# Weight low parts on VectorE, a later chunk load and a new step order in a retention and two-layer kernel

## The chip, the cores and the metric

One Trainium2 chip, one core of it. The metric is the device time of one execution in microseconds (us); of the kernel before, three executions gave 586.96 us as median, 585.64 as lowest and 587.08 as highest.

## What is computed

A retention layer (batch 2, 8 heads, 768 positions, head size 64), its output laid out as 1536 tokens of 512 numbers, and then two feed-forward layers of width 2048 one behind the other, the first with Mish, the second with ELU. q, k and v are float32; the four weight matrices arrive as float64. Cut to what matters:

```python
state = gamma[h] * state + outer(k[t], v[t])       # for each t, per batch and head
y[t] = scale * q[t] @ state
x = y.transpose(0, 2, 1, 3).reshape(1536, 512)
h = x @ w_in;  x = (h * tanh(log1p(exp(h)))) @ w_out          # moe: Mish
h = x @ w_in2; out = where(h > 0, h, exp(min(h, 0)) - 1) @ w_out2   # moe2: ELU
```

## The kernel before

**Retention.** The 768 positions of both batches are cut into 12 chunks of 128 (numbers 0 to 11, batches alternating). Chunks 0 to 3 go through `scores`, `attend` and `add_state` ahead of the main loop. Chunks 4 to 11 go through `scores64` (scores of the chunk and the new states) and `attend64` (output of the chunk), each of which issues its TensorE matmuls and returns a function `rest` that issues the work of VectorE and ScalarE behind them. For each chunk GpSimd makes a scaled k (`scale_k`, L187, tile kd) that `scores64` needs and a scaled q (`scale_q`, L202, tile qd) that `attend64` needs. From chunk 4 on there is one buffer for kd and one for qd.

**Feed-forward.** The tokens are 3 blocks of 512; each layer has 16 chunks of 128 hidden units; so there are 2 x 3 x 16 = 96 tiles. Step n of the main loop issues `up(n)` (L396: 12 matmuls 128x512, into tile h) and `down(n - 3)` (L453: 12 matmuls into the accumulators a), with the activation between them. All products are made from high and low parts: hi times hi, lo times hi, hi times lo. Steps 0 to 4 also carry the scores and outputs of chunks 4 to 7, because from step 6 on `up` needs block 1, which is made of these four chunks:

| step | TensorE in order |
|---|---|
| 0 | up(0), scores64 of chunk 4 |
| 1 | up(1), attend64 of 4, scores64 of 5 |
| 2 | up(2), attend64 of 5, scores64 of 6 |
| 3 | up(3), attend64 of 6, down(0), scores64 of 7 |
| 4 | up(4), attend64 of 7, down(1) |

**Weights.** Each of the 64 weight halves is fetched as raw 64-bit words (`fetch`, L109, tile st, four buffers), turned into float32 by two ScalarE operations (`dec_fields`, L116 and L118) and two VectorE operations (`dec_join`, L127 and L133), and then split by `dec_split`: ScalarE copies the high part (L146, tiles w0h, w1h), GpSimd subtracts to get the low part (L147, tiles w0l, w1l). `dec_join` issues the fetch of the half that takes the freed buffer. w0 is what `up` needs, w1 what `down` needs.

**Order.** The program's order is written out by hand; each engine works through its own instructions in that order, and each waits at its head for what it needs. All DMAs are issued by SyncE (SP) in one queue, with eight completion semaphores in turn. What matters below: on VectorE the order of the parts of steps 0 to 4; on GpSimd the order of kd, qd and low parts; on SP the order of chunk loads (`load_chunk`: L167 qk, L172 kv), decay tables (`load_tab`: L208) and weight halves.

"Half 3" below is the weight half with place 3 in the order of need; "kd of chunk 6" is what `scale_k(6)` writes.

Of the kernel before, what the change touches and what calls it, by code (L numbers as in the profile page):

```python
# [9 lines left out]
F32 = mybir.dt.float32  # L10
# [4 lines left out]
ALU = mybir.AluOpType  # L15
# [8 lines left out]
NCH = B * CPB  # L24
# [11 lines left out]
LAG = 3  # L36
# [7 lines left out]
def retention_then_two_ffn(  # L44
# [7 lines left out]
    nc = tc.nc  # L52
# [86 lines left out]
    def dec_split(k):  # L139
        f = parts.pop(k)  # L140
        n, i = halves[k]
        pl = late["w"] if n % (GRP + EXTRA) >= GRP else wpool
        hi, lo = wt[n, i] = tuple(
            pl.tile([P, HC], F32R, tag=f"w{i}{z}", name=f"w{i}{z}") for z in "hl"
        )
        nc.scalar.copy(out=hi, in_=f)  # L146
        nc.gpsimd.tensor_tensor(out=lo, in0=f, in1=hi.bitcast(F32), op=ALU.subtract)  # L147


    ct = const.tile([P, N_CT], F32, name="ct")  # L150
# [14 lines left out]
    def load_qk(c):  # L165
        t = qk_p.tile([P, 2, NPAIR, P], F32, tag="qk", name="qk")
        nc.sync.dma_start(out=t.rearrange("p a j t -> p (a j t)"), in_=qkv[c, :, :2 * DM])  # L167
        return t

    def load_kv(c):  # L170
        t = kv_p.tile([P, 2, H, D], F32, tag="kv", name="kv")
        nc.sync.dma_start(out=t.rearrange("p a h d -> p (a h d)"), in_=qkv[c, :, 2 * DM:])  # L172
        return t

    def load_chunk(c):
        raw[c] = (load_qk(c), load_kv(c))
# [28 lines left out]
    def load_tab(i):  # L205
        tabs[i] = qd_p.tile([P, NPAIR, P], F32, tag="tab", name="tab", bufs=2)
        at = N_CT + (i - 2) * N_TQ
        nc.sync.dma_start(  # L208
            out=tabs[i].rearrange("p j t -> p (j t)"), in_=consts[:, at:at + N_TQ]
        )  # L210
# [176 lines left out]
    hs, es, gs, accs, acc_ps = {}, {}, {}, {}, {}  # L387
# [24 lines left out]
    def mish(n):  # L412
        h = hs.pop(n)
        gh = gpool.tile([P, TB], F32R, tag="gh", name="gh")
        gl = gpool.tile([P, TB], F32R, tag="gl", name="gl")
        nc.scalar.activation(out=gh, in_=h, func=AF.Mish)  # L416
        nc.scalar.activation(out=h, in_=h, func=AF.Mish)  # L417
        nc.vector.tensor_tensor(out=gl, in0=h, in1=gh.bitcast(F32), op=ALU.subtract)  # L418
        gs[n] = (gh, gl)

    def elu_a(n):
        h = hs[n]
# [62 lines left out]
    with tc.manual_schedule():  # L485
        nc.scalar.preload_act_table_set("mish")
        for s in states:
            nc.vector.memset(s, 0.0)
        qk0 = load_qk(0)
        nc.sync.dma_start(out=ct[:, :N_MASK], in_=consts[:, :N_MASK])  # L490
        raw[0] = (qk0, load_kv(0))
        qk1 = load_qk(1)
        nc.sync.dma_start(out=ct[:, N_MASK:], in_=consts[:, N_MASK:N_CT])
        raw[1] = (qk1, load_kv(1))
        for c, tag in ((2, "xh1"), (3, "xl1")):
            both = xpool.tile([P, KT, TB], F32R, tag=tag, name=tag).bitcast(F32)
            qk, kv = (both[:, 2 * a:2 * a + 2] for a in range(2))
            nc.sync.dma_start(
                out=qk.rearrange("p a n -> p (a n)"), in_=qkv[c, :, :2 * DM]
            )  # L500
            raw[c] = (
                qk.rearrange("p a (j t) -> p a j t", t=P),
                kv.rearrange("p a (h d) -> p a h d", d=D),
            )
        def load_early_kv(c):
            nc.sync.dma_start(
                out=raw[c][1].rearrange("p a h d -> p (a h d)"), in_=qkv[c, :, 2 * DM:]
            )

        fetch()  # L510
        load_early_kv(2)
        load_early_kv(3)
        fetch()
        started = done = 0
        N = len(tiles)

        def room(k, now):
            if k >= NHALF:
                return False
            n, i = halves[k]  # L520
            old = n - GRP - (EXTRA if "w" in late else 0)
            return old < 0 or last_use[old] + LAG * i <= now

        ta, th, tb = ("a0", "a1"), ("h", "h"), ("a2", "a3")
        for i in range(3):
            warm = psa.tile([P, NPAIR, P], F32, tag=f"a{i}", name="warm")
            nc.tensor.matmul(warm, states[0][:, 0], states[0], start=True, stop=True)
        scale_k(0)
        scores(0, ta)()
        scale_k(1)  # L530
        scores(1, th)()
        for c, tags in ((0, tb), (1, th)):
            rests = attend(c, tags[0]), add_state(c, tags[1])
            for rest in rests:
                rest()
        load_chunk(4)
        fetch()
        load_chunk(5)
        load_tab(2)
        fetch()  # L540
        load_chunk(6)
        scale_q(2)
        scale_q(3)
        scores(2, ta)()
        scores(3, th)()
        dec_fields(0)
        dec_join(0)
        scale_k(2)

        lower = mask[half[1]].rearrange("p r j t -> p (r j) t")  # L550
        nc.gpsimd.tensor_copy(lower[:, :, half[0]], lower[:, :, half[1]])
        scale_k(3)
        rests = attend(2, tb[0]), attend(3, tb[1]), add_state(2, "h"), add_state(3, "h")
        rests[0]()
        dec_split(0)
        rests[1]()
        dec_fields(1)
        dec_join(1)
        scale_k(CPT)
        dec_split(1)  # L560
        rests[2]()
        rests[3]()
        dec_fields(2)
        scale_q(CPT)
        dec_join(2)
        done, joined, started, credit = 2, 3, 3, 0.0

        load_tab(3)
        steps = {0: [(scores64, 4, ta)], 3: [(attend64, 6), (scores64, 7)], 4: [(attend64, 7)]}
        for n in (1, 2):  # L570
            steps[n] = [(attend64, n + 3, tb), (scores64, n + 4, ta)]
        for c in range(2 * CPT, NCH):
            n = FIRST + 2 * (c - 2 * CPT)
            steps[n], steps[n + 1] = [(scores64, c)], [(attend64, c)]
        for n in range(N + LAG):
            todo = steps.get(n, [])
            rests = []
            if n < N:
                up(n)
                if todo:  # L580
                    f, *args = todo[0]
                    rests.append(f(*args))
            full = down(n - LAG) if n >= LAG else []
            for f, *args in todo[1:]:
                rests.append(f(*args))
            first_layer = n < N and tiles[n][0] == 0
            if first_layer:
                mish(n)
            elif n < N:
                elu_a(n)  # L590
            if 1 <= n <= N and tiles[n - 1][0] == 1:
                elu_b(n - 1)
            if full and not full[0][1]:
                for e in full:
                    evacuate(*e)
            for (f, c, *_), rest in zip(todo, rests):
                if f is scores64 and c + 1 < NCH:
                    scale_k(c + 1)
                rest()
                if f is attend64 and c + 3 < NCH:  # L600
                    load_chunk(c + 3)
                if f is attend64 and c + 1 < NCH:
                    scale_q(c + 1)
                    if c % B and (c + 1) // B + 1 < CPB:
                        load_tab((c + 1) // B + 1)
            for k in range(done, joined):
                dec_split(k)
            done = joined
            if full and full[0][1]:
                for e in full:  # L610
                    evacuate(*e)
            if 1 <= n <= N and tiles[n - 1][0] == 1:
                split(n - 1)
            if any(f is attend64 and c == NCH - 1 for f, c, *_ in todo):
                actx.close()
                late["acc"] = ctx.enter_context(pool("acc12", 1))
                late["m"] = ctx.enter_context(pool("tmp2", 2))
                late["w"] = ctx.enter_context(pool("w2", EXTRA))
            if later:
                later.pop(0)()  # L620
            dec_join(*range(joined, started))
            joined = started
            ahead = range(started, min(started + 2 * GRP, NHALF))
            credit += max([1.0] + [
                (k - started + 1) / max(need[k] - n - 2, 0.5) for k in ahead
            ])
            credit = min(credit, 2.0)
            while credit >= 1 and room(started, n):
                dec_fields(started)
                started += 1  # L630
                credit -= 1


def _consts():
# [54 lines left out]
```

## Time and profile before

| | |
|---|---|
| median of 3 executions | 586.96 us (585.64 to 587.08) |
| the profiled execution | 587.08 us, its span 585.3 us, granted clock 0.994 |
| TensorE (PE) busy | 568.0 us, 97% of the span |
| VectorE (DVE) busy | 320.4 us, 55% |
| ScalarE (ACT) busy | 282.1 us, 48% |
| GpSimd (POOL) busy | 201.6 us, 34% |

The span runs from the first to the last instruction, and what the time has beyond it (1.8 us) lies around it. An engine's busy time leaves out what its sequencer does. PEclk is the share of full speed that TensorE was granted. The profile also says of an instruction how long its engine was idle before it and what ended that.

### The profile page before, as it was taken

What the parts mean: (1) busy time and instruction counts of PE and PEld (TensorE: products, weight loads), DVE (VectorE), ACT (ScalarE), POOL (GpSimd) and SP (SyncE); (2) the same over time, 40 slices, a digit from 0 to 9 for tenths busy, and PEclk for the clock granted to TensorE, in tenths of its full rate; (3) what the DMA queues carried; (4) which work ended last, traced back from release to release, by engine and by line L of the source; (5) the groups of instructions that cost most, each with busy time, mean ns of one, the idle gap of its engine ahead of it and who ended that gap; (6) DMA issues with size and microseconds to landing.
All of it is one profiled execution on the core that took longest, in us unless ns stands there. A gap on an engine that the chain in (4) does not pass through costs nothing.

```text
span 585.3 us, 8785 instructions
## 1 busy us (share of the span) xinstructions
PE 568.0 (97%) x3510; PEld 466.5 (80%) x3510; DVE 320.4 (55%) x432; ACT 282.1 (48%) x506; POOL 201.6 (34%) x151
## 2 busy tenths in 40 slices
PE   7967999999999999999999999999999999999997
PEld 5756788888888888888888888888888888888885
DVE  3857755432655553310775996234797774534524
ACT  1555546344654652222665684434875753233331
POOL 2644433301222222110361595221565552222221
PEclk9988999999999999999999999999999999999999
DMA  8968642202242332000233232000333100100101
GB/s 326 394 237 271 199 144 74 74 1 72 77 140 76 106 108 73 0 1 0 97 120 109 72 108 73 1 0 1 109 109 108 37 0 1 72 1 0 73 0 72
DMA packets 15304, 51.70 MB, mean 88 GB/s; under 512 B 1696, under 2 KB 1696, under 8 KB 15264
## 3 DMA queue, kind: packets, MB, share of 16 engines
q1 hardware_dynamic: 15264, 51.15, 25.1%
q8 instruction: 27, 0.44, 0.3%
q14 instruction: 13, 0.11, 0.1%
HBM read 48.00 MB, written 3.15 MB: 87 GB/s over the span
## 4 chain that ended last, share of the span: by engine, by line
PE 88%; DVE 1%; POOL 0%; ACT 0%; issue 0%; POOLq 0%
PE a L453 44%; PE h L396 43%; PE y L348 1%; DVE acc L466 0%; PE y L355 0%; PE sc L304 0%; PE sc L311 0%; POOL w0l L147 0%; DVE y L370 0%; DVE xl L374 0%; ACT t L367 0%; ACT xh L372 0%; POOLq L147 0%
## 5 line engine op out<-in xcount | busy, mean ns | idle before, releaser
L396 PE MATMUL h<-xh,w0h 128*128 128x512 f32 x384 | 103.8, 392 | 2.5 <-ACT w0h L146 2.5
L409 POOL TENSOR_TENSOR gl<-m,gh 128x512 fp32r<-128x512 f32 x48 | 69.6, 1449 | 106.1 <-ACT gh L408 106.1
L396 PE MATMUL h<-xh,w0l 128*128 128x512 f32 x384 | 103.9, 393 | 2.0 <-POOL w0l L147 1.9
L418 DVE TENSOR_TENSOR gl<-h,gh 128x512 fp32r<-128x512 f32 x48 | 33.2, 691 | 130.8 <-ACT h L417 126.9
L396 PE MATMUL h<-xl,w0h 128*128 128x512 f32 x384 | 103.0, 390 | 0.0
L426 ACT ACTIVATE e<-c 128x512 f32<-128x512 f32 x48 | 30.4, 633 | 123.3 <-DVE c L425 123.3
L147 POOL TENSOR_TENSOR w0l<-f,w0h 128x512 fp32r<-128x512 f32 x32 | 42.7, 1337 | 135.1 <-ACT w0h L146 126.0
L425 DVE TENSOR_SCALAR c<-h 128x512 f32<-128x512 f32 x48 | 33.1, 690 | 101.8 <-PE h L396 101.7
L416 ACT ACTIVATE gh<-h 128x512 fp32r<-128x512 f32 x48 | 28.6, 597 | 121.3 <-PE h L396 121.3
L396 PEld LDWEIGHTS h<-xh,w0l 128*128 128x128 f32 x384 | 72.2, 189 | 18.5 <-POOL w0l L147 3.7
L396 PEld LDWEIGHTS h<-xh,w0h 128*128 128x128 f32 x384 | 71.8, 188 | 17.9 <-ACT w0h L146 3.0
L396 PEld LDWEIGHTS h<-xl,w0h 128*128 128x128 f32 x384 | 72.5, 189 | 15.3
L453 PE MATMUL a<-gh,w1h 128*128 128x512 f32 x192 | 75.8, 395 | 0.0
L453 PE MATMUL a<-gl,w1h 128*128 128x512 f32 x192 | 74.8, 390 | 0.0
L453 PE MATMUL a<-gh,w1l 128*128 128x512 f32 x192 | 74.8, 390 | 0.0
L453 PE MATMUL a<-w1h,gh 128*128 128x512 f32 x192 | 74.7, 389 | 0.0
L453 PE MATMUL a<-w1l,gh 128*128 128x512 f32 x192 | 74.7, 389 | 0.0
L453 PE MATMUL a<-w1h,gl 128*128 128x512 f32 x192 | 74.7, 389 | 0.0
L133 DVE SCALAR_TENSOR_TENSOR f<-f,st 128x512 int32<-128x512 int32 x64 | 69.7, 1098 | 3.8
L127 DVE SCALAR_TENSOR_TENSOR st<-st 128x512 int32<-128x512 int32 x64 | 71.3, 1123 | 0.6 <-ACT st L118 0.6
L147 POOL TENSOR_TENSOR w1l<-f,w1h 128x512 fp32r<-128x512 f32 x32 | 45.7, 1429 | 61.5 <-ACT w1h L146 48.4
L116 ACT ACTIVATE f<-st 128x512 f32<-128x512 f32 x64 | 42.8, 668 | 10.1 <-DMA st<-w 6.2
(80 smaller groups left out, 691.8 us busy)
## 6 DMA issues: line engine op xcount, KB each, us to landing
st<-w SPq DMA_DIRECT2D x64, 512.0 KB, 3.6
qk<-qkv SPq DMA_DIRECT2D x10, 512.0 KB, 7.6
kv<-qkv SPq DMA_DIRECT2D x10, 512.0 KB, 8.2
out<-acc SPq DMA_DIRECT2D x12, 256.0 KB, 2.1
xh<-qkv SPq DMA_DIRECT2D x2, 512.0 KB, 9.4
xl<-qkv SPq DMA_DIRECT2D x2, 512.0 KB, 10.0
tab<-consts SPq DMA_DIRECT2D x4, 256.0 KB, 8.6
ct<-consts SPq DMA_DIRECT2D x1, 512.0 KB, 5.7
```

The source lines that it names most:

```text
L116: nc.scalar.activation(out=f, in_=t[:, :, 1].bitcast(F32), func=AF.Copy, scale=2.0 ** -112)
L127: nc.vector.scalar_tensor_tensor(out=t[:, :, 1], in0=t[:, :, 1], scalar=-(2 ** 31), in1=t[:, :, 0], op0=ALU.bitwise_and, op1=ALU.bitwise_or,)
L133: nc.vector.scalar_tensor_tensor(out=f, in0=f, scalar=3, in1=t[:, :, 1], op0=ALU.logical_shift_left, op1=ALU.bitwise_or,)
L147: nc.gpsimd.tensor_tensor(out=lo, in0=f, in1=hi.bitcast(F32), op=ALU.subtract)
L348: nc.tensor.matmul(y[r][sl, far, j], state[m][sl, j], qd[sl, j, half[m]], start=j == 0 and far == 1, stop=far == 1, skip_group_check=True,)
L396: nc.tensor.matmul(h, u[:, k * P:(k + 1) * P], v[:, k], start=i == 0, stop=i == len(passes) - 1)
L409: nc.gpsimd.tensor_tensor(out=gl, in0=g, in1=gh.bitcast(F32), op=ALU.subtract)
L416: nc.scalar.activation(out=gh, in_=h, func=AF.Mish)
L418: nc.vector.tensor_tensor(out=gl, in0=h, in1=gh.bitcast(F32), op=ALU.subtract)
L425: nc.vector.tensor_scalar(out=c, in0=h, scalar1=0.0, scalar2=None, op0=ALU.min)
L426: nc.scalar.activation(out=e, in_=c, func=AF.Exp)
L453: nc.tensor.matmul(a, l, r, start=first and i == 0, stop=last and i == 2)
```

## The change

Five edits. (1) The low parts of weights (L147) are made by VectorE in place of GpSimd. (2) `mish` no longer issues the low part of its result at once but hands it back; the loop issues it behind the chunk steps, except in a later step that carries two of them. (3) In steps 0 to 2 the chunk steps' `rest` functions, with the `scale_k`, `scale_q` that go with them, are issued in reversed order: `scores64` ahead of `attend64`. (4) The load of chunk 6, and decay table 3 with it, moves from ahead of the loop to the end of step 0. (5) The other chunk loads move from behind their `attend64` to the end of the step.

```diff
@@ dec_split
-        nc.gpsimd.tensor_tensor(out=lo, in0=f, in1=hi.bitcast(F32), op=ALU.subtract)
+        nc.vector.tensor_tensor(out=lo, in0=f, in1=hi.bitcast(F32), op=ALU.subtract)
@@ mish
-        nc.vector.tensor_tensor(out=gl, in0=h, in1=gh.bitcast(F32), op=ALU.subtract)
-        gs[n] = (gh, gl)
+        def rest():
+            nc.vector.tensor_tensor(out=gl, in0=h, in1=gh.bitcast(F32), op=ALU.subtract)
+            gs[n] = (gh, gl)
+        return rest
@@ ahead of the loop
         load_tab(2)
         fetch()
-        load_chunk(6)
...
-        load_tab(3)
@@ in the loop over n
-                mish(n)
+                low = mish(n)
...
-            for (f, c, *_), rest in zip(todo, rests):
+            pairs = list(zip(todo, rests))
+            if n < LAG:
+                pairs.reverse()
+            elif first_layer and len(todo) > 1:
+                low()
+                low = None
+            for (f, c, *_), rest in pairs:
                 if f is scores64 and c + 1 < NCH:
                     scale_k(c + 1)
                 rest()
-                if f is attend64 and c + 3 < NCH:
-                    load_chunk(c + 3)
                 if f is attend64 and c + 1 < NCH:
                     scale_q(c + 1)
                     if c % B and (c + 1) // B + 1 < CPB:
                         load_tab((c + 1) // B + 1)
+            if first_layer and low:
+                low()
             for k in range(done, joined):
                 dec_split(k)
...
+            if n == 0:
+                load_chunk(6)
+                load_tab(3)
+            for f, c, *_ in todo:
+                if f is attend64 and c + 3 < NCH:
+                    load_chunk(c + 3)
```

What this does to the order on the engines shows at three places. In all of them a name's number is that of its buffer or load.

GpSimd, from the start of the main loop. Before: low parts w0l stand between kd and qd. The kd rows are those of chunks 5, 6 and 7, the qd rows those of chunks 4, 5 and 6.

```order
L202 TENSOR_TENSOR qd_338<-qk_206,tab_216 128x512
L187 TENSOR_TENSOR kd_398<-kv_214,ct_94 128x512
L147 TENSOR_TENSOR w0l_406<-f_335,w0h_405 128x512
L202 TENSOR_TENSOR qd_516<-qk_212,tab_216 128x512
L187 TENSOR_TENSOR kd_518<-kv_222,ct_94 128x512
L202 TENSOR_TENSOR qd_638<-qk_220,tab_344 128x512
L187 TENSOR_TENSOR kd_642<-kv_514,ct_94 128x512
```

The same place now, for the same chunks:

```order
L202 TENSOR_TENSOR qd_334<-qk_206,tab_216 128x512
L187 TENSOR_TENSOR kd_391<-kv_214,ct_94 128x512
L187 TENSOR_TENSOR kd_500<-kv_411,ct_94 128x512
L202 TENSOR_TENSOR qd_518<-qk_212,tab_216 128x512
L187 TENSOR_TENSOR kd_624<-kv_537,ct_94 128x512
L202 TENSOR_TENSOR qd_640<-qk_409,tab_413 128x512
```

The low part is gone, and qd of chunk 5 stands behind kd of chunk 6, qd of chunk 6 behind kd of chunk 7: each kd waits for the kv load of its chunk.

SP's queue, from the fetch of half 3 on. Before, chunk 6 (qk_220, kv_222) is loaded right behind it and chunk 7 (qk_512, kv_514) ahead of halves 7 and 8.

```order
L109 DMA st_218<-w 128x1024
L167 DMA qk_220<-qkv 128x1024
L172 DMA kv_222<-qkv 128x1024
L109 DMA st_259<-w 128x1024
L109 DMA st_323<-w 128x1024
L109 DMA st_342<-w 128x1024
L208 DMA tab_344<-consts 128x512
L167 DMA qk_512<-qkv 128x1024
L172 DMA kv_514<-qkv 128x1024
L109 DMA st_528<-w 128x1024
L109 DMA st_531<-w 128x1024
```

Now:

```order
L109 DMA st_218<-w 128x1024
L109 DMA st_255<-w 128x1024
L109 DMA st_319<-w 128x1024
L109 DMA st_338<-w 128x1024
L167 DMA qk_409<-qkv 128x1024
L172 DMA kv_411<-qkv 128x1024
L208 DMA tab_413<-consts 128x512
L109 DMA st_524<-w 128x1024
L109 DMA st_527<-w 128x1024
L167 DMA qk_535<-qkv 128x1024
L172 DMA kv_537<-qkv 128x1024
```

Chunk 6 now stands behind halves 4, 5 and 6, and chunk 7 behind halves 7 and 8, whose fetches wait until VectorE has joined halves 3 and 4 in step 1.

VectorE, from the join of half 1 to the first scores of step 0 (at). Before:

```order
L133 SCALAR_TENSOR_TENSOR f_318<-f_318,st_122 128x512
L277 TENSOR_TENSOR compact0_97<-st_292,state0_95 64x256 x2
L277 TENSOR_TENSOR compact1_98<-st_301,state1_96 64x256 x2
L127 SCALAR_TENSOR_TENSOR st_210<-st_210 128x512
L133 SCALAR_TENSOR_TENSOR f_335<-f_335,st_210 128x512
L418 TENSOR_TENSOR gl_394<-h_346,gh_393 128x512
L319 TENSOR_TENSOR at_400<-sc_359,ct_94 128x256
```

Now:

```order
L133 SCALAR_TENSOR_TENSOR f_314<-f_314,st_122 128x512
L147 TENSOR_TENSOR w0l_324<-f_314,w0h_323 128x512
L277 TENSOR_TENSOR compact0_97<-st_288,state0_95 64x256 x2
L277 TENSOR_TENSOR compact1_98<-st_297,state1_96 64x256 x2
L127 SCALAR_TENSOR_TENSOR st_210<-st_210 128x512
L133 SCALAR_TENSOR_TENSOR f_331<-f_331,st_210 128x512
L319 TENSOR_TENSOR at_393<-sc_353,ct_94 128x256
```

The low part of half 1 stands ahead of the states and of the join of half 2, and Mish's low part no longer stands ahead of at.

## Rows read from the trace of the kernel before

**Rows 1.** Busy time by stretch; columns are in the header line.
```profile
core 0: us, PE busy (x) PEld busy (x) DVE busy (x) ACT busy (x) POOL busy (x), PEclk, DMA share, GB/s
30.00:32.00 2.00, 2.00 (x114) 1.93 (x110) 0.00 (x0) 0.03 (x1) 2.00 (x2) 1.00 1.03 412
...
34.90:42.70 7.80, 3.81 (x125) 3.84 (x127) 7.23 (x14) 5.21 (x12) 1.31 (x1) 0.78 0.28 102
...
39.00:42.50 3.50, 3.50 (x113) 3.50 (x116) 3.50 (x5) 2.11 (x5) 1.31 (x1) 0.52 0.11 26
...
45.50:49.50 4.00, 4.00 (x11) 2.92 (x12) 3.96 (x7) 2.04 (x4) 2.50 (x2) 0.57 0.96 252
...
80.00:575.00 495.00, 495.00 (x2552) 409.15 (x2552) 264.75 (x339) 244.47 (x434) 164.37 (x117) 1.00 0.18 59
```

**Rows 2.** Waits, 0 to 100 us: total us, times, longest.
```profile
PE y L348 <- DVE state L326: 5.0, 2, 4.1
PE h L396 <- ACT w0h L146: 2.5, 1, 2.5
...
PE h L396 <- POOL w0l L147: 1.9, 2, 1.4
```

**Rows 3.** Groups by line and shape, VectorE: busy us, mean ns.
```profile
L127 DVE SCALAR_TENSOR_TENSOR st<-st 128x512 int32<-128x512 int32 x64 | 71.3, 1123 | 0.6 <-ACT st L118 0.6
L133 DVE SCALAR_TENSOR_TENSOR f<-f,st 128x512 int32<-128x512 int32 x64 | 69.7, 1098 | 3.8
...
L418 DVE TENSOR_TENSOR gl<-h,gh 128x512 fp32r<-128x512 f32 x48 | 33.2, 691 | 130.8 <-ACT h L417 126.9 <-PE sc L311 3.8
```

**Rows 4.** Timeline of GpSimd: start, duration, idle before.
```profile
22.57 1.05 POOL L187 TENSOR_TENSOR kd<-kv,ct 128x512 f32<-128x512 f32 x1 [1.02 <-DMA kv<-qkv]
...
27.55 1.29 POOL L202 TENSOR_TENSOR qd<-qk,tab 128x512 f32<-128x512 f32 x1 [1.36 <-DMA tab<-consts]
```

**Rows 5.** Timeline of VectorE.
```profile
22.59 1.57 DVE L133 SCALAR_TENSOR_TENSOR f<-f,st 128x512 int32<-128x512 int32 x1
24.08 1.72 DVE L277 TENSOR_TENSOR compact<-st,state 64x256 f32<-64x256 f32 x4
...
26.77 0.69 DVE L133 SCALAR_TENSOR_TENSOR f<-f,st 128x512 int32<-128x512 int32 x1
...
28.77 0.41 DVE L326 TENSOR_TENSOR state<-sc,compact 128x256 f32<-128x256 f32 x1
```

**Rows 6.** Timeline of all engines, steps 0 to 3.
```profile
24.19 0.62 ACT L146 CAST w0h<-f 128x512 fp32r<-128x512 f32 x1 [2.36 <-DVE f L133]
...
29.32 0.24 PE L348 MATMUL y<-qd,state 64*64 64x64 f32 x1 [0.98 <-DVE state L326]
...
31.21 0.66 PE L311 MATMUL sc<-kv,kd 64*64 64x64 f32 x31
...
38.89 0.24 PE L348 MATMUL y<-qd,state 64*64 64x64 f32 x1 [4.05 <-DVE state L326]
...
50.02 0.27 PE L348 MATMUL y<-qd,compact 64*64 64x64 f32 x1
```

**Rows 7.** Timeline of SP's queue: issues (x2: the pair's start).
```profile
41.07 2.03 SPq L109 DMA_DIRECT2D st<-w  x2
...
43.66 0.38 SPq L172 DMA_DIRECT2D kv<-qkv  x1
...
49.81 0.93 SPq L109 DMA_DIRECT2D st<-w  x2
...
52.13 0.38 SPq L172 DMA_DIRECT2D kv<-qkv  x1
```

**Rows 8.** DMA issues at 41.1, 43.7 and 52.1: size, us to landing.
```profile
st<-w SPq DMA_DIRECT2D x1, 512.0 KB, 3.5
...
kv<-qkv SPq DMA_DIRECT2D x1, 512.0 KB, 8.5
...
kv<-qkv SPq DMA_DIRECT2D x1, 512.0 KB, 6.6
```

## Prediction

> **What bounds the kernel now.** I read the busy time by stretch first: from 80 to 575 us TensorE is busy for all of 495 us at full clock, while VectorE has 264.75 us of work there [rows 1]. So nothing in the main part waits for VectorE or GpSimd, and the change is decided before 80 us. Next the waits of TensorE in the first 100 us: 5.0 us for the states that VectorE makes, 2.5 us for a high part of weights, 1.9 us for low parts from GpSimd [rows 2], 9.4 us in all that a better order could win. The timeline says where: attend64 of chunk 5 idles 4.05 us before it starts at 38.89, because VectorE had the rest of chunk 4's output ahead of chunk 5's states; attend64 of chunk 6 starts at 50.02 [rows 6]. Twice the clock drops: 0.52 from 39.0 to 42.5, 0.57 from 45.5 to 49.5, each right behind a TensorE idle stretch of 4.05 and 2.5 us [rows 1, 2, 6]. The prediction follows the starts of the chunk outputs, 29.32, 38.89 and 50.02, into the changed order.
>
> **The change part by part.**
>
> *Low parts on VectorE.* 64 instructions of 128x512. No row shows this form on VectorE; the nearest are 691 ns for a subtraction that reads one operand from PSUM, and 1098 to 1123 ns, the means of the two joins, which read two operands from SBUF [rows 3]. I take 0.69 us alone, and 1.1 us as the upper bound. The joins show what the gap is: one of them takes 0.69 us alone, and 1.57 us where a GpSimd operation (1.05 us from 22.57) started just before it: it ended 0.54 us behind that one's end [rows 4, 5]. So a VectorE instruction with two SBUF operands waits out a GpSimd instruction that started first. In the main part VectorE gets 64 x 0.69 = 44 us and gives back up to 64 x (0.43 + 0.41) = 54 us of such waiting, as GpSimd has less to do. I cost it at nothing there: what hides it is TensorE's 495 us against 265 of VectorE. That cover would be gone only if VectorE nearly doubled.
>
> *The same, ahead of chunk 4.* The low part of half 1 waits for ScalarE's copy, which ends at 24.19 + 0.62 = 24.81 [rows 6]. On VectorE the low part then runs to 25.5, and behind it stand the four state operations (1.72 us, which began at 24.08 [rows 5]), now to 27.2, and the join of half 2. Its first half ends at 27.8, but GpSimd's qd of chunk 4 asks at 27.55, when its table lands [rows 4], and starts before the second half can: 27.8 + 1.29 = 29.1, and the second half ends 0.54 us later, at 29.6, where before it ended at 26.77 + 0.69 = 27.46 [rows 5]. That is 2.1 us late. Mish's low part no longer stands behind it (0.69 us won), so attend64 of chunk 4 starts at about 30.75 and not at 29.32: 1.4 us later.
>
> The Trainium skill's page "SBUF — State Buffer", section "Who interferes with whom", has this as a rule: a VectorE instruction with two SBUF inputs contends with a GpSimd instruction that reads SBUF, and the later one blocks until the first is through. The trace agrees (1.57 us against 0.69). It speaks against this change, since every low part on VectorE now has two SBUF inputs. By the rule this piece is worth 1.4 us; if the second half went first, it would be 0.3 us and the sum below 1.1 us lower.
>
> *Reversed chunk steps.* The states of chunk 5 no longer wait for chunk 4's output. Before, scores64 of chunk 5 ended at 31.21 + 0.66 = 31.87 [rows 6], now 1.4 us later, at 33.3; VectorE can make the states (1.5 us) by 34.9; up(2) ended at 38.89 - 4.05 = 34.84, now 36.2. The 4.05 us wait for VectorE is gone. What is late next: qd of chunk 5 stands behind kd of chunk 6 on GpSimd, and that waits for kv of chunk 6.
>
> *Chunk 6 behind halves 4 to 6.* The fetch of half 6 waits for the join of half 2, so SP issues it at 29.65, and qk and kv of chunk 6 behind it. A lone transfer lands 3.5 us after its issue [rows 8]. With 412 GB/s [rows 1] each further 512 KB takes 1.27 us, so kv lands at 29.65 + 3.5 + 2.5 = 35.7 at best. Then kd (1.05) and qd (1.29) [rows 4]: attend64 of chunk 5 starts at 38.2 at best. Later bursts were slower: kv was the fourth transfer, and landed 43.66 + 8.5 - 41.07 = 11.1 and 52.13 + 6.6 - 49.81 = 8.9 us after the first issue [rows 7, 8], where the full rate would give 3.5 + 3.8 = 7.3. With such a delay attend64 starts at about 40. I take 39, so as before: the wait of 4 us is turned into one for qd.
>
> *Chunk 7 behind halves 7 and 8.* These fetches wait for VectorE's joins of halves 3 and 4 in step 1. The work in front of them (states, chunk 4's output, Mish's low part, the joins) is the same set that VectorE worked through from 34.9 to 42.7, 7.23 us busy in 7.8 [rows 1]. It now begins at 33.35 and takes about 7.5 us, so the second join ends at 40.85, the first at 40.2, and SP issues half 7 then (41.07 before [rows 7]). kv of chunk 7 is the fourth transfer: 7.3 us later at full rate, 8.9 and 11.1 by the two bursts. I take 10.0, the mean of the bursts, since this burst too starts from an idle queue: 50.2. GpSimd then makes kd of chunk 7 and only behind it qd of chunk 6: 50.2 + 0.1 + 1.05 + 1.29 = 52.6. So attend64 of chunk 6 starts at 52.6 and not at 50.02: **2.6 us later**. up(3) ended by 50.02 before, part of it at half clock, and nothing in front of it starts later now; so qd sets the start, and what up(3) wins is lost in front of attend64.
>
> *Behind that.* Low parts of up(4) and up(5) cost 1.9 us of waiting [rows 2]. In step 3 VectorE still has the states of chunk 7 ahead of them, in step 4 only 0.69 us of Mish: I take 0.7 us of the 1.9 as won, 0 and 1.9 as bounds. TensorE idles for 3 to 4 us ahead of attend64 of chunk 6; behind both earlier stops of that size about 3.4 us ran at half clock, which would cost 1.7 us here, or nothing if the stop is shorter. I take 0.4.
>
> **Sum.** 2.6 - 0.7 + 0.4 = +2.3 us on the profiled execution's 587.08 us (span 585.3 and 1.8 around it): **589.4 us**. The profiled execution lies 0.12 us above the median, which I leave aside.
>
> **Rivals.**
>
> 1. *The loads are in time and the removed waits are removed (faster).* If the join of half 2 were not held up by qd, everything from 29.3 on is 1.1 to 1.4 us earlier, and with a burst at full rate kv of chunk 7 lands at 39 + 7.3 = 46.3 and attend64 of chunk 6 starts at 48.7, 1.3 us earlier; with 0.7 to 1.9 us of low parts won and no half clock behind it, the sum is -2.0 to -3.2 us: 584.3. For it: 9.4 us of waits on VectorE, ScalarE and GpSimd that the new order attacks, all seen in the rows. Against it: both conditions have to hold, and a queue that lands 512 KB at 1.27 us is seen only in the first 35 us.
>
> 2. *The new wait is there, but short (no change).* The join is late as I say, but the burst runs at the full rate: kv of chunk 7 at 40.2 + 7.3 = 47.5, attend64 of chunk 6 at 49.9, so 0.1 us earlier, and 0.7 us won behind it: 586.3. It decides against my forecast when the fourth transfer lands less than about 8.3 us after the first issue.
>
> 3. *VectorE becomes the bound of the main part (slower).* Per weight half it now has two joins and a low part, 3 x 0.69 = 2.07 us alone, against 1.12 + 1.10 = 2.22 us before [rows 3]; so its load hardly grows, and a loss would need most of its instructions to collide with GpSimd. At 0.4 us more for each of 64 low parts it is 26 us of VectorE time in 495, still under the cover. I give it little.
>
> **How the numbers follow.** About 0.3%, 1.8 us, is what a measurement of this kernel can tell from no change: same is 585.2 to 588.7 us. Chances: the forecast (a late qd of chunk 6) 0.52, rival 1 0.20, rival 2 0.26, rival 3 0.02. So slower 0.54, same 0.26, faster 0.20. The forecast's own range goes from 588.0 (burst of 8.9 us) to 592 (11.1 us, an issue up to 1 us later because kd or qd of GpSimd holds up the joins of halves 3 and 4, and the full 1.7 us of half clock). With the other cases the range is 584.3 to 592.0; a win beyond rival 1's -3 us and a loss beyond 5 us are left out.
>
> **What would show it.** In the changed profile attend64 of chunks 5 and 6 (L348) should wait for POOL qd (L202), and POOL kd (L187) for the DMA kv, at about 35 and 50 us. The join of half 2 (third L133) should take about 1.7 us and end near 29.6. attend64 should start near 30.7, 39 and 52.6. Half 7 should be fetched at 40.2, and kv of chunk 7 land near 50. L147 on VectorE should take 0.69 us or a little more in the mean, the two joins fewer than 1.0 us, and TensorE should stay full from 80 to 575. I am wrong if attend64 of chunk 6 starts before 49.5, or if TensorE shows idle time behind 80 us.

## The result and the profile after

The changed kernel takes 592.31 us (median of 4, 591.56 to 594.39) against 586.3 us (585.47 to 587.08) of the kernel before on the same chip: 1.0103 times the time, interval [1.0082, 1.0123]. It is slower, as forecast, but by 6.0 us in the medians where 2.3 were forecast, and outside the range. The profiled execution took 591.56 us (span 589.8), 4.5 us over that of before (587.08); the working below is against that pair. The rest of the 6.0 us lies in which executions were profiled: that of the changed kernel is its fastest, 0.75 us under its median, and that of before lies 0.78 us over its own. The other three executions of the changed kernel took 0.3 to 2.8 us longer at a granted clock of 0.987 to 0.988 (0.991 in the profiled one, 0.994 before); where they lost it is not shown.

The waits of TensorE in the changed kernel, 0 to 100 us (total, times, longest) and, behind the dots, 85 to 589 us:

```profile
PE y L348 <- POOL qd L202: 6.6, 2, 5.3
PE h L396 <- ACT w0h L146: 3.7, 1, 3.7
...
PE h L396 <- DVE w0l L147: 1.1, 1, 1.1
...
PE a L457 <- ACT acc L467: 2.1, 1, 2.1
```

Beside [rows 2]: the 5.0 us for states became 6.6 us for qd, the wait for a high part grew from 2.5 to 3.7, that for low parts shrank from 1.9 to 1.1. The last line has no counterpart before: TensorE now waits in the main part, at 466 us, once.

So the loss has two pieces. up(6), the first tile of block 1, starts at 73.32 us and before at 71.25: **2.07 us** are lost in steps 0 to 5. From there to up start 444.72 (442.65 before) the distance stays 2.07; the tile that starts at 475.29 before starts at 479.80 now, 4.51 later: **2.44 us** more, lost at the end of a block of the second layer (16 steps on the same 512 tokens).

**The early piece.** The changed kernel's timeline, TensorE, GpSimd, VectorE and ScalarE; in brackets the idle time before a row and what ended it:

```profile
22.66 0.69 DVE L133 SCALAR_TENSOR_TENSOR f<-f,st 128x512 int32<-128x512 int32 x1
24.04 0.85 DVE L147 TENSOR_TENSOR w0l<-f,w0h 128x512 fp32r<-128x512 f32 x1 [0.69 <-ACT w0h L146]
...
27.29 0.69 DVE L133 SCALAR_TENSOR_TENSOR f<-f,st 128x512 int32<-128x512 int32 x1
...
28.02 1.27 POOL L202 TENSOR_TENSOR qd<-qk,tab 128x512 f32<-128x512 f32 x1 [3.68 <-DMA tab<-consts]
...
29.35 0.27 PE L348 MATMUL y<-qd,state 64*64 64x64 f32 x1 [1.31 <-POOL qd L202]
...
37.17 1.23 POOL L187 TENSOR_TENSOR kd<-kv,ct 128x512 f32<-128x512 f32 x1 [6.88 <-DMA kv<-qkv]
38.36 1.71 POOL L202 TENSOR_TENSOR qd<-qk,tab 128x512 f32<-128x512 f32 x1
...
40.12 0.37 PE L348 MATMUL y<-qd,state 64*64 64x64 f32 x1 [5.28 <-POOL qd L202]
...
43.05 0.76 ACT L367 COPY t<-y 64x256 f32<-64x256 f32 x2 [4.73 <-PE y L355]
...
44.70 0.75 DVE L319 TENSOR_TENSOR at<-sc,ct 128x256 f32<-128x256 f32 x2 [4.09 <-PE sc L311]
...
46.26 0.88 DVE L370 TENSOR_TENSOR y<-y,t 64x256 f32<-64x256 f32 x2
...
47.71 0.63 ACT L146 CAST w0h<-f 128x512 fp32r<-128x512 f32 x1
...
48.39 1.93 PE L396 MATMUL h<-xh,w0h 128*128 128x512 f32 x4 [3.74 <-ACT w0h L146]
...
49.90 1.14 POOL L187 TENSOR_TENSOR kd<-kv,ct 128x512 f32<-128x512 f32 x1 [9.83 <-DMA kv<-qkv]
51.00 1.73 POOL L202 TENSOR_TENSOR qd<-qk,tab 128x512 f32<-128x512 f32 x1
...
52.94 0.27 PE L348 MATMUL y<-qd,compact 64*64 64x64 f32 x1
```

attend64 of chunk 4 starts at 29.35, as before (29.32 [rows 6]). TensorE idles 5.28 us ahead of attend64 of chunk 5, for qd, which stands behind a kd that waited 6.88 us for its load. The scores of chunk 6 come later with it, VectorE waits 4.09 us for them, and behind its states and chunk 5's output ScalarE makes the high part of half 3 only at 47.71; so up(3) starts at 48.39 (45.43 before). The reversed order adds to that: ScalarE had copied chunk 5's output by 43.81 (t), but VectorE's next operation on it (y) stands behind the states of chunk 6 and starts at 46.26; before, y came ahead of those states, at 43.30. No kernel below undoes the reversal alone, so its price is not measured. attend64 of chunk 6 starts at 52.94 (50.02 before [rows 6]): up(3)'s matmuls end just then, and qd, ending at 52.73, is hardly ahead of them.

**The late piece.** Busy time from 430 to 480 us (columns as in [rows 1]); the kernel before:

```profile
430.00:480.00 50.00, 50.00 (x222) 41.42 (x221) 41.27 (x47) 32.81 (x58) 27.20 (x19) 1.00 0.19 64
```

and the changed kernel:

```profile
430.00:480.00 50.00, 47.85 (x211) 39.33 (x210) 42.48 (x53) 31.91 (x57) 10.58 (x9) 1.00 0.24 74
```

VectorE was already busy for 41 of 50 us here, where the 495 us of the main part gave 264.75 [rows 1]. One step of this stretch in the changed kernel (c, L429, is the first VectorE operation on a tile of `up`), then the block's end:

```profile
441.07 0.68 DVE L429 TENSOR_SCALAR c<-h 128x512 f32<-128x512 f32 x1
...
441.79 0.63 ACT L430 ACTIVATE e<-c 128x512 f32<-128x512 f32 x1 [2.15 <-DVE c L429]
...
442.99 0.60 ACT L146 CAST w0h<-f 128x512 fp32r<-128x512 f32 x1
...
443.63 0.69 DVE L147 TENSOR_TENSOR w0l<-f,w0h 128x512 fp32r<-128x512 f32 x1 [0.56 <-ACT w0h L146]
...
444.19 1.30 POOL L409 TENSOR_TENSOR gl<-m,gh 128x512 fp32r<-128x512 f32 x1 [4.31 <-ACT gh L408]
444.24 1.81 DVE L127 SCALAR_TENSOR_TENSOR st<-st 128x512 int32<-128x512 int32 x1
...
446.08 0.69 DVE L133 SCALAR_TENSOR_TENSOR f<-f,st 128x512 int32<-128x512 int32 x1
...
446.69 0.68 DVE L429 TENSOR_SCALAR c<-h 128x512 f32<-128x512 f32 x1
...
465.45 2.03 ACT L467 COPY acc<-a 128x512 f32<-128x512 f32 x4
...
466.07 0.50 PE L457 MATMUL a<-w1h,gh 128*128 128x512 f32 x1 [2.15 <-ACT acc L467]
```

From c to c it is 5.61 or 5.62 us, and TensorE needs 5.44 for a tile (32.64 us for six, 442.65 to 475.29 before). The step is a ring: ScalarE waits 2.15 us for c, makes the high part only behind its two operations on it, VectorE waits 0.56 us for that high part, GpSimd's gl then holds up the join (1.81 us where 0.69 is its time alone, ending 0.56 us behind gl, as in [rows 4, 5]), and the next c is late. At the block's end ScalarE's copies of the accumulators stand behind its late work, and TensorE, which needs the accumulators, stops for 2.15 us.

The groups of VectorE over the whole execution, changed kernel (busy us, mean ns):

```profile
L127 DVE SCALAR_TENSOR_TENSOR st<-st 128x512 int32<-128x512 int32 x64 | 69.1, 1088 | 0.7 <-ACT st L118 0.7
L133 DVE SCALAR_TENSOR_TENSOR f<-f,st 128x512 int32<-128x512 int32 x64 | 48.7, 770 | 1.7
...
L147 DVE TENSOR_TENSOR w0l<-f,w0h 128x512 fp32r<-128x512 f32 x32 | 22.2, 695 | 15.5 <-ACT w0h L146 15.4
L147 DVE TENSOR_TENSOR w1l<-f,w1h 128x512 fp32r<-128x512 f32 x32 | 21.9, 685 | 6.6 <-ACT w1h L146 6.6
```

Beside [rows 3], L133 gave back 21.0 us and L127 2.2. The low parts cost 44.1 us of work, as reckoned, and in the third column 22.0 us of waiting for ScalarE, which the reckoning did not have.

### The profile page after: what moved, and what is told of

Same layout as the page of the kernel before. It is cut to its first block, busy times and chain, and to the rows that moved or that the text cites. A ratio compares the mean times of both kernels' runs of the same rounds, so it can differ in the third digit from the quotient of the medians.

```text
span 589.8 us, 8635 instructions
## 1 busy us (share of the span) xinstructions
PE 569.9 (97%) x3510; PEld 467.6 (79%) x3510; DVE 332.6 (56%) x496; ACT 282.4 (48%) x506; POOL 108.3 (18%) x87
## 4 chain that ended last, share of the span: by engine, by line
PE 84%; DVE 7%; DMA 4%; ACT 3%; POOL 1%; issue 0%; SPq 0%; POOLq 0%
PE a L457 40%; PE h L396 40%; DVE st L127 2%; DMA kv<-qkv 2%; DMA xl<-qkv 2%; PE y L348 1%; DVE f L133 1%; ACT e L430 1%; ACT c L431 1%; DVE c L429 1%; PE sc L304 1%; DVE w0l L147 1%; PE y L355 1%; PE sc L311 1%; ACT w0h L146 1%; DVE acc L470 0%
## 5 line engine op out<-in xcount | busy, mean ns | idle before, releaser
L409 POOL TENSOR_TENSOR gl<-m,gh 128x512 fp32r<-128x512 f32 x48 | 63.2, 1316 | 206.8 <-ACT gh L408 202.5
L429 DVE TENSOR_SCALAR c<-h 128x512 f32<-128x512 f32 x48 | 33.0, 687 | 75.0 <-PE h L396 75.0
L127 DVE SCALAR_TENSOR_TENSOR st<-st 128x512 int32<-128x512 int32 x64 | 69.1, 1088 | 0.7 <-ACT st L118 0.7
L487 POOL TENSOR_TENSOR xl<-acc,xh 128x512 fp32r<-128x512 f32 x12 | 17.4, 1450 | 180.2 <-ACT xh L486 176.6
L133 DVE SCALAR_TENSOR_TENSOR f<-f,st 128x512 int32<-128x512 int32 x64 | 48.7, 770 | 1.7
L457 PEld LDWEIGHTS a<-w1h,gh 128*128 128x128 f32 x192 | 36.0, 188 | 10.1 <-ACT acc L467 2.6
```

Of the source, the lines that this page charges most:

```text
L127: nc.vector.scalar_tensor_tensor(out=t[:, :, 1], in0=t[:, :, 1], scalar=-(2 ** 31), in1=t[:, :, 0], op0=ALU.bitwise_and, op1=ALU.bitwise_or,)
L133: nc.vector.scalar_tensor_tensor(out=f, in0=f, scalar=3, in1=t[:, :, 1], op0=ALU.logical_shift_left, op1=ALU.bitwise_or,)
L409: nc.gpsimd.tensor_tensor(out=gl, in0=g, in1=gh.bitcast(F32), op=ALU.subtract)
L429: nc.vector.tensor_scalar(out=c, in0=h, scalar1=0.0, scalar2=None, op0=ALU.min)
L457: nc.tensor.matmul(a, l, r, start=first and i == 0, stop=last and i == 2)
L487: nc.gpsimd.tensor_tensor(out=xl, in0=s, in1=xh.bitcast(F32), op=ALU.subtract)
```

## The experiments

Each was timed beside the kernel before on the same chip, in three groups on three chips: the first four below against 586.67 us; qd ahead of kd, the two kernels with exchanged tags and the first with the splits against 586.39; the other four against 587.07. In the traces up(0) starts between 20.7 and 21.4 us (20.96 before, 20.80 in the changed kernel), so starts in different kernels compare to some tenths of a microsecond. In kernels that choose the engine of the low part in a line of their own, the later lines are numbered one higher (L397 is `up`).

**Low parts by layer.** Two kernels split edit (1). The changed kernel with the low parts of the second layer on GpSimd:

```diff
-        nc.vector.tensor_tensor(out=lo, in0=f, in1=hi.bitcast(F32), op=ALU.subtract)
+        eng = nc.vector if n < NFC else nc.gpsimd
+        eng.tensor_tensor(out=lo, in0=f, in1=hi.bitcast(F32), op=ALU.subtract)
```

> The changed kernel, with the low parts of the second layer's weights made by GpSimd again (first layer: VectorE). Ring theory: the loss of 6 us has two pieces, 2.1 us before 70 us (late loads, GpSimd's order) and 2.4 us or more at about 466 us, where TensorE waits for ScalarE's accumulator copies because in the second layer VectorE's low part waits for ScalarE and its join behind it for GpSimd, 5.61 us a step against TensorE's 5.44. So here the wait at 466 us is gone, the part before 70 us stays +2, and the time is 588.5 to 590. Rival (load: VectorE's extra work as such, or all of the loss before 80 us): 591.5 to 592.5, as the change.

The kernel before with only the low parts of the second layer on VectorE (the same line with `n >= NFC`):

> The kernel before, with the low parts of the second layer's weights alone made by VectorE. Ring theory: nothing changes before 80 us, one wait of TensorE for ScalarE's accumulator copies of 2 to 4 us appears in the second layer, and the time is 2.4 to 4 us above before (588.5 to 590.5). Rival (all of the loss is in the first 80 us): no difference from before, no wait there.

The first took 589.79 us, 1.0071 [1.0044, 1.0097], TensorE waits for nothing behind 85 us, and up(6) starts at 73.39. The second took 589.77 us, 1.0053 [1.0033, 1.0073], its early part is that of before (up(6) at 71.54), and it has the stop: 2.15 us at 464.29. The late piece belongs to the low parts of the second layer, alone and in either kernel. In the medians each of the two lies 3.1 us over before, 6.2 in sum, as the whole change does with 6.0. The start of c in the first of the two:

```profile
442.27 0.69 DVE L430 TENSOR_SCALAR c<-h 128x512 f32<-128x512 f32 x1 [0.99 <-PE h L397]
447.71 0.69 DVE L430 TENSOR_SCALAR c<-h 128x512 f32<-128x512 f32 x1 [0.98 <-PE h L397]
```

In that kernel VectorE has 0.98 us to spare per tile of 5.44. In the changed kernel the low part asks for 0.61 us of its time (start to start) and 0.56 of waiting. That is 1.17, so 0.19 too much: 5.63, where 5.61 was measured.

**Lock or load.** The changed kernel with gl of the second layer on VectorE too, so that GpSimd has nothing there and VectorE has more:

```diff
-        nc.gpsimd.tensor_tensor(out=gl, in0=g, in1=gh.bitcast(F32), op=ALU.subtract)
+        nc.vector.tensor_tensor(out=gl, in0=g, in1=gh.bitcast(F32), op=ALU.subtract)
```

> The changed kernel, with the second layer's low part of the activation (gl, 48 subtractions of 128x512) also on VectorE, so that GpSimd no longer takes part in the second layer's steps. Ring theory: the join no longer waits for GpSimd, a step of the ring shrinks from 5.61 to about 5.0 us, the wait at 466 us goes although VectorE has 33 us more to do: 588.5 to 590. Rival (VectorE's load as such): the wait grows, 593 to 600.

589.87 us, 1.0061 [1.0037, 1.0084], and no stop of TensorE in the main part. The changed kernel's c from the block's start, and the low part in its first step:

```profile
415.00 0.69 DVE L429 TENSOR_SCALAR c<-h 128x512 f32<-128x512 f32 x1 [2.10 <-PE h L396]
...
419.51 0.69 DVE L147 TENSOR_TENSOR w0l<-f,w0h 128x512 fp32r<-128x512 f32 x1 [2.50 <-ACT w0h L146]
...
423.65 0.68 DVE L429 TENSOR_SCALAR c<-h 128x512 f32<-128x512 f32 x1
...
457.92 0.68 DVE L429 TENSOR_SCALAR c<-h 128x512 f32<-128x512 f32 x1
463.54 0.68 DVE L429 TENSOR_SCALAR c<-h 128x512 f32<-128x512 f32 x1
```

and with gl on VectorE:

```profile
415.33 0.69 DVE L429 TENSOR_SCALAR c<-h 128x512 f32<-128x512 f32 x1 [0.66 <-PE h L396]
423.45 0.68 DVE L429 TENSOR_SCALAR c<-h 128x512 f32<-128x512 f32 x1
...
454.64 0.68 DVE L429 TENSOR_SCALAR c<-h 128x512 f32<-128x512 f32 x1
459.74 0.68 DVE L429 TENSOR_SCALAR c<-h 128x512 f32<-128x512 f32 x1
```

Counted in steps of 5.44 us from the first row, both are about 3 us late at 423.5: in the block's first step ScalarE copies accumulators ahead of the high part, and VectorE waits 2.50 us for that at the low part, with the joins behind it. With GpSimd silent the step is then 5.10 us, below TensorE's 5.44, and VectorE catches up, from 2.9 us late at 429.15 to 0.9 at 459.74; with the lock it is 5.61 and VectorE falls from 4.0 us late (429.84) to 5.0 (463.54). So the six ring steps add only 1.1 of these 5.0 us, and the block's first step 3.2; what the lock decides is that VectorE can't work them off. That makes the stop, not the number of VectorE's operations: the kernel that doesn't stop has 48 more.

**Chunk loads.** The changed kernel with edits (4) and (5) undone (chunks 6 and 7 and table 3 loaded where they were):

```diff
+        load_chunk(6)
...
+                if f is attend64 and c + 3 < NCH:
+                    load_chunk(c + 3)
...
-            if n == 0:
-                load_chunk(6)
-                load_tab(3)
-            for f, c, *_ in todo:
-                if f is attend64 and c + 3 < NCH:
-                    load_chunk(c + 3)
```

> The changed kernel, with all chunk loads and decay table 3 back where the kernel before has them. Theory of the late loads: kv of chunk 6 lands near 31 us and that of chunk 7 near 38.5, qd of chunk 5 is ready by 34.5 and attend64 of chunk 5 starts at 35 to 36 in place of 40.1; attend64 of chunk 6 starts at 44 to 47 in place of 52.9; the time before 70 us falls by 4 to 7 us, that at 466 us stays: 585 to 588. Rival (the reversed order or VectorE's own order costs it): attend64 of chunk 6 stays above 49 and the time above 590.

590.46 us, 1.0064 [1.0039, 1.009]. up(6) starts at 71.22, as before, and the stop of 2.15 us at 464 stays: without the late loads the early piece is gone. But the gain that the theory expected did not come, and the signs of the rival did: attend64 of chunk 6 started at 50.81, not at 44 to 47, and the time is above 590. attend64 of chunk 5 came at 37.48, not at 35 to 36; it waited 2.99 us for xl (the low part) of chunk 4's output, whose banks in PSUM, the memory that matmuls write to, it takes over. That is 1.41 us earlier than before, but up(3) starts 0.36 us later than before (45.79), behind a wait of 3.55 us for its high part. What the early loads win at chunk 5 is lost again in front of up(3).

**Order of kd and qd.** The changed kernel, loads still late, but GpSimd makes qd ahead of kd:

```diff
             for f, c, *_ in pairs:
-                if f is scores64 and c + 1 < NCH:
-                    scale_k(c + 1)
                 rest()
+            for f, c, *_ in todo:
+                if f is scores64 and c + 1 < NCH:
+                    scale_k(c + 1)
                 if f is attend64 and c + 1 < NCH:
                     scale_q(c + 1)
```

> The changed kernel with one edit: in a step of the first block GpSimd makes qd of the next chunk output first and kd of the next scores behind it (before this edit kd, then qd). Chunk 6 is still fetched late (its kv lands at about 37). Theory (the early loss of 2.1 us is qd of chunk 5 queued behind kd of chunk 6, which waits for kv of chunk 6): attend64 of chunk 5 no longer starts at 40.1 but at about 37.5, where the kernel with early loads had it, now ended by another wait than qd; scores64 of chunk 6 waits for kd until about 38.5; up(6) starts 1 to 2 us earlier than 73.3; the second loss stays (TensorE waits about 2 us for ScalarE's copy near 464); the whole 590 to 591. Rival (what counts is when the load itself lands, through chunk 6's own scores and states): up(6) stays at 73 or later and the whole at 592.

588.63 us, 1.0056 [1.0035, 1.0076]. Its TensorE waits:

```profile
35.71 0.29 PE L348 MATMUL y<-qd,state 64*64 64x64 f32 x2 [0.58 <-DVE xl L374]
44.41 2.08 PE L396 MATMUL h<-xh,w0h 128*128 128x512 f32 x4 [5.57 <-ACT w0h L146]
```

attend64 of chunk 5 starts at 35.71 and up(6) at 69.23, 4.1 us earlier than in the changed kernel and 2.0 earlier than before, with the loads as late as they were (kd waits for kv until 36.83), and more than the 1 to 2 us expected. The early piece needs both, a late load and a qd queued behind the kd that waits for it; the lateness alone does not cost it. The 2.16 us for ScalarE's copy remain (at 461.99).

**Both causes away.** The last kernel with the second layer's low parts on GpSimd:

> The changed kernel with both suspected causes taken away: qd of the next output ahead of kd on GpSimd, and the low parts of the second layer on GpSimd again; loads, reversed steps and first-layer low parts stay as changed. Theory (two causes, in two stages, that add): up(6) starts at about 69.2 to 70 as with the reordering alone (73.3 in the changed kernel, 71.25 before), TensorE doesn't wait near 464, and the time is 585 to 587, so no slower than before. Rival (a third cause, or one that comes back once the other is gone): 588 or more, with a wait that neither kernel showed.

585.24 us, 0.9985 [0.9962, 1.0007]: no slower than before. up(6) starts at 68.43, and nothing waits in the main part. The two causes account for the loss. What remains is the wait of up(3) for its high part (3.73 us at 43.64).

**Loads and order alone.** The changed kernel with edit (1) undone (all low parts on GpSimd):

> The changed kernel with all low parts on GpSimd again, so only the loads and the order of steps are changed. Theory (the low parts cost only in the second layer; the early loss is the order and the loads): up(6) at 73 to 74, no wait near 464, 589 to 590, as with the second layer's low parts alone on GpSimd (589.8). Rival (the first layer's low parts on VectorE gain or cost time in front of chunk 6): up(6) more than 1 us from 73.4.

594.33 us, 1.0129 [1.0113, 1.0145], no faster than the whole change, against the theory: up(6) starts only at 79.14, 5.75 us behind the kernel that differs in the first layer's low parts. Its GpSimd and TensorE:

```profile
49.51 1.04 POOL L187 TENSOR_TENSOR kd<-kv,ct 128x512 f32<-128x512 f32 x1 [9.96 <-DMA kv<-qkv]
50.51 1.71 POOL L202 TENSOR_TENSOR qd<-qk,tab 128x512 f32<-128x512 f32 x1
52.19 1.71 POOL L147 TENSOR_TENSOR w0l<-f,w0h 128x512 fp32r<-128x512 f32 x1
...
53.95 2.07 PE L396 MATMUL h<-xh,w0l 128*128 128x512 f32 x4 [3.98 <-POOL w0l L147]
```

On GpSimd the low part of up(3) stands behind the kd and qd that wait for chunk 7. So with these loads VectorE is the better place for it in the first layer, and it is the worse one in the second.

**Trying for a gain.** Four kernels attack what the traces left. First the PSUM banks: the low parts as in the first experiment, loads early, and the tags of step 2 (they name the PSUM banks that a chunk step takes) exchanged.

```diff
-        for n in (1, 2):
-            steps[n] = [(attend64, n + 3, tb), (scores64, n + 4, ta)]
+        steps[1] = [(attend64, 4, tb), (scores64, 5, ta)]
+        steps[2] = [(attend64, 5, ta), (scores64, 6, tb)]
```

> Low parts of the second layer on GpSimd again, chunk loads where they were in the kernel before, and in step 2 the PSUM tags of chunk 5's output and chunk 6's scores exchanged. With the loads early and the tags as they are, attend64 of chunk 5 started at 37.5 with a wait of 3.0 us. Theory (that rest is the reuse of the two PSUM banks of chunk 4's output, which VectorE reads only behind ScalarE's copy of half 4): with the other banks attend64 of chunk 5 starts at 35 to 36 behind up(2), with no wait of over 1 us, and up(6) starts 1 to 2 us before 71.2. Rival (VectorE's order sets it, whichever bank): start stays at 37 to 38 and up(6) at 71.2. By both there is no wait of TensorE near 464; time by the theory 584 to 586, by the rival 587.

attend64 of chunk 5 starts at 34.68, right behind up(2), so the banks did hold it; but up(3) then waits 7.31 us for its high part, up(6) starts at 72.20, and the time is 588.28 us, 1.003 [1.0013, 1.0047]. Neither the theory nor the rival had that: the wait was only moved. That leaves ScalarE's order, in which the high part of half 3 stands behind xh of chunk 5's output. The splits ahead of the chunk steps' rests, chunk 6 loaded behind half 4:

```diff
+            if 2 <= n <= 4:
+                for k in range(done, joined):
+                    dec_split(k)
+                done = joined
             pairs = list(zip(todo, rests))
```

> Low parts of the second layer on GpSimd, chunk 6 loaded behind half 4 only, the other loads as in the kernel before, and in steps 2 to 4 the splits (high parts on ScalarE, low parts) placed ahead of the chunk steps' rests. Theory (the 3.7 us wait of up(3) for the high part of its half is ScalarE's order: the copy stands behind xh of chunk 5): the wait of up(3) falls under 0.5 us, up(3) starts at about 43 and up(6) at about 69 to 70; 584 to 586 us. Rival (TensorE then waits for something else, chunk 6's states or chunk 7's load, for as long): up(6) stays at 71 and the time at 587 to 588.

582.68 us, 0.9947 [0.9923, 0.9971]: faster than both kernels. Its TensorE:

```profile
35.47 0.33 PE L349 MATMUL y<-qd,state 64*64 64x64 f32 x2 [0.72 <-POOL qd L203]
38.90 1.19 PE L397 MATMUL h<-xh,w0h 128*128 128x512 f32 x4 [0.68 <-ACT w0h L146]
42.23 0.27 PE L349 MATMUL y<-qd,compact 64*64 64x64 f32 x1 [0.31 <-POOL qd L203]
49.84 0.63 PE L305 MATMUL sc<-qk 64*64 64x64 f32 x27 [2.80 <-DVE gl L421]
```

The wait of up(3) fell to 0.68 us, and up(6) starts at 65.72, more than 3 us earlier than expected. What TensorE waits for now is ahead of the scores of chunk 7 (2.80 us). With the tags exchanged as well:

> The last kernel and in step 2 the PSUM tags of chunk 5's output and chunk 6's scores exchanged as well: low parts of the second layer on GpSimd, splits ahead of rests in steps 2 to 4. Theory (both waits, the banks of chunk 4's output and ScalarE's order, are real and separate): attend64 of chunk 5 at 35 to 36, up(3) without a wait over 0.5 us, up(6) at 67 to 69, the time 581 to 584. Rival (the next thing behind both, chunk 6's states or chunk 7's load, sets the end): up(6) as with the splits alone, within 0.5 us.

582.79 us, 0.995 [0.9925, 0.9975], up(6) at 66.89: nothing won. attend64 of chunk 5 starts at 35.28, and at 35.47 without the exchange; the banks no longer hold it once chunk 6 stands behind half 4. The same splits in the kernel of "both causes away":

> The last kernel with the splits (high and low parts) of steps 2 to 4 ahead of the chunk steps' rests. Theory (the 5.6 us in front of up(3) that was left is ScalarE's order: the high part of half 3 stands behind xh of chunk 5, and that behind the states of chunk 6): the high part is made at about 38.5 and up(3) waits only for the joins of VectorE, to about 40.5 to 41.5; up(6) at 65 to 67; 581 to 584 us, with the late load of chunk 6 still in it. Rival (chunk 6, which comes late, then sets it in another place, attend64 or scores64 of chunks 6 and 7): up(6) at 68 or later, 585 or more.

583.57 us, 0.9944 [0.9927, 0.9962], up(6) at 67.04, and 1.7 us under that kernel. And the splits, with the first layer's low parts, in the kernel before:

> The kernel before with two edits: low parts of the first layer on VectorE, and the splits of steps 2 to 4 ahead of the chunk steps' rests; loads and order of chunk steps as before. Theory (the gain of the kernel with splits first comes from ScalarE's order alone): the 2.45 us in front of up(3) goes, the 4.05 us in front of attend64 of chunk 5 stays; up(6) at 68.5 to 69.5, 584 to 585. Rival (it needs the reversed steps too, without which half clock follows the stop at 35 to 39): up(6) at 70.5 to 71.5, 586 to 587.

584.58 us, 0.9962 [0.9948, 0.9977], up(6) at 69.32: a gain of 2.5 us over before, of the 3.7 with splits first, needs none of the reversed steps. How much of it is ScalarE's order and how much the first layer's low parts is open, since these were not moved alone. The 4.05 us did not stay where they were: the stop is now in front of chunk 4's output (3.47 us, at 31.27), and chunk 5's idles 0.66.

## Why the prediction was wrong

- **The step that failed** is "I cost it at nothing there", of the low parts in the main part, with its reason, "TensorE's 495 us against 265 of VectorE", and "that cover would be gone only if VectorE nearly doubled". It measured +2.44 us. The 44 us of work were right, and the joins gave back 23 of the 54 us allowed; only L133 fell under the 1.0 us looked for (0.77), L127 stayed at 1.09. Wrong was the mean: in 430 to 480 us VectorE was busy for 41.27 of 50, with 0.98 us to spare per tile, and a low part there brings a wait for ScalarE with it, 0.56 us in a step and 2.50 at the block's start. Rival 3 had the place but priced it by the sum of work, asked for collisions of most instructions where one per step was enough, and got 0.02.
- **The sum of the early part** was +2.3 and measured +2.07, in part by luck: errors in its terms cancelled, as the next points show. With the late piece added to it, the forecast would have been 591.8 against 591.56 for the profiled execution.
- **The main mechanism** (qd behind a kd that waits for its load) held, and making qd first won 4.1 us of up(6)'s start. But the delay came in at chunk 5, where I took 39 and the trace has 40.12. kv of chunk 6 was issued at 28.98 and landed 8.0 us later, at 37.0, where the best case had 35.7; kd and qd then took 2.90 us beside VectorE's joins and not 2.34. For chunk 6 qd tied with up(3), and the forecast of 52.6 met the measured 52.94 by luck: half 7 was issued at 39.01 and not at 40.2, kd started 10.9 us behind that and not 10.1, and kd and qd took 2.83 us and not 2.34.
- **"Nothing in front of it starts later now"**, of up(3), failed: up(3) started 2.96 us later, since ScalarE's high part stood behind states and output that had become late. Its matmuls alone put attend64 of chunk 6 at about 52.9.
- **The join of half 2 held up to 29.6** did not happen. kv of chunk 5 came later, so kd no longer collided with the join of half 1 (0.69 us at 22.66, 1.57 before [rows 5]); the low part came 0.77 us earlier than reckoned, and the join of half 2 ended at 27.98, 0.04 us ahead of qd. The 1.4 us charged to attend64 of chunk 4 were 0.03. So the work ahead of half 7's fetch began at 31.94 and not at 33.35, and the fetch came early.
- **Behind attend64 of chunk 6** low-part waits went from 1.9 to 1.1 us: 0.8 won, forecast 0.7. The 0.4 us for half clock there were nothing: TensorE's stop was ahead of up(3), not of attend64, and the granted clock was 1.00 from 53 to 60 us. What the trace of before could not show is that the loads and the order alone would have cost far more: without the first layer's low parts on VectorE up(6) starts at 79.14.
- **A slip in rival 1**: -2.0 to -3.2 us give 583.9 to 585.1 us, so its 584.3, the lower end of the range, is a point inside its own sum.

## What to carry to other kernels

Cost an edit in the stage where it runs, by the spare time of one step of that stage: 0.98 us per tile was the number, not 495 against 265. Where an instruction is moved to an engine, list what it waits for there and who then waits for its new engine; a ring over three engines that is 0.17 us too long per step leaves no room to work off a delay from the block's start, and shows nothing until the block's end asks for all of it at once. And on an in-order engine put what is ready (qd, a high part) ahead of what waits: qd first brought up(6) forward by 4.1 us and the splits took 1.7 us off the median, where bringing the load itself forward moved up(6) by only 2.1.

## What the runs showed of the hardware

The lock between VectorE and GpSimd lengthens both sides. L133 of two halves took 1.28 us (53.21) without GpSimd beside it and 3.20 us (37.42) while kd and qd ran, and that qd took 1.71 us where 1.27 was its time alone. The Trainium skill's page "SBUF — State Buffer", section "Who interferes with whom", calls the ports that the two engines share an exclusive lock, and has the order of issue decide who blocks. The single collisions agree (1.81 us at 444.24, ending 0.56 us behind gl); qd's 1.71 us shows that in a row of them GpSimd waits as well. In the second layer's steps the lock costs the same whichever half of a join it meets: L127 and L133 took 0.69 and 1.80 us (447.50 and 448.22) before, and 1.81 and 0.69 (444.24 and 446.08) after. Before, GpSimd's low part was the partner (448.18); with the low parts gone gl is (444.19), so taking one GpSimd operation of two away did not take the lock away.
